# A decode step's backward pass: every engine's instruction order replaced, with four key/value gradient stores moved to GpSimd's queue

## Chip, core and metric

One core of one Trainium2 chip. The metric is the device time of one execution in microseconds (us); the kernel before has a median of 482.54 us in three runs (481.98 to 483.42).

## What is computed

The reference is the forward and backward pass of one decode step: an attention block with cached keys and values beside a gated bilinear block, both on the same normalised input of 2 rows (B = 2, D = 576).

```python
xn = _layernorm(x)
q = xn @ wq                                  # 32 query heads of 128, 16 key/value heads
p = softmax(q k^T * 128 ** -0.5)             # 4096 cached positions
out = x + (p v) @ wo + ((xn @ w_gate) * (xn @ w_up)) @ w_down
return out, *vjp(out)(grad_out)              # for x, k_cache, v_cache, wq, wo, w_gate, w_up, w_down
```

With one query per row there is little arithmetic. The caches are 32 heads of 1 MB each for keys and as many for values (bf16); they are read once, and their gradients, of the same size, are written once. The weights (576 x 4096, 4096 x 576, three of 576 x 4608) are read once, and their gradients written once.

## The kernel before

**Work.** A *step* `s` (16 of them) takes two key/value heads of one batch row: two K heads and two V heads are loaded, 1 MB each, into `big` tiles of 128 x 4096. A *group* is two steps (both batch rows of the same two heads); it needs a slice of `wq` and of `wo` and stores a slice of their gradients. Beside them run 9 *slices* of the bilinear block, 512 columns each, with loads of gate, up (tile `gu`, a single buffer) and down weights (tile `ww`).

In a step, by line: VectorE turns each head in blocks of 32 x 32 (`turn`, L421); TensorE forms the scores from K (`score`, L1105, t = 0), the softmax follows (L1171 to L1198), and V gives the gradient of the probabilities (L1105, t = 1) and from it the gradient of the scores (L1226 to L1237). GpSimd builds block-diagonal tiles `BD` from the query and from the gradient of the output (L1093, three buffers). `head_outer` multiplies them with the probabilities (dV, `out_3`) or with the score gradients (dK, `out_2`) on TensorE (L1127); each 128 x 1024 result is moved from PSUM by ScalarE (L425) or VectorE (L427), an *eviction*, and four of them fill a `big` tile, which one 1 MB DMA stores (`put`, L654). `contract` multiplies the probabilities with V and the score gradients with K (L1282). At a group's end `group_back` makes the gradients of `wq` and `wo` and adds to the sums `acc` and `accx` (L937, L962); after the last group `final_dx` turns `accx` into the input's gradient `out_1` (L1365 to L1389), and a DMA of 2 KB stores it (L1330).

**DMA.** Loads of K and V and of the down weights, and stores of dK and dV, are issued by SP (queue q1); the other weight loads and all stores of weight gradients by GpSimd, POOL in the profile (queue q0). The K and V loads of the last two steps are GpSimd's too. The two queues feed the same 16 DMA engines.

**Order.** The order of every engine's instructions is worked out by `Order` while the program is built. Each piece of work is a generator that asks for engines, buffers and DMAs, with a cost for each request; of the requests that can start within `SLACK` of the earliest on an engine, the one with the lowest priority number is taken. Priorities are `pr(name, s) = 28 s + PR[name]`, with offsets `HEAD` and `TAIL` for the first and last two steps. `EV` gives each eviction to ScalarE or VectorE, whichever would end first, with `BIAS` against VectorE. Class `Lines` models the two DMA queues as one server each, and `gate`s hold weight loads back until a given K or V load has been issued. The costs thus change nothing but the order: every wait on the chip is on a real semaphore, and an engine whose next instruction waits holds all that stand behind it. Each of the two kinds of queue has eight DMA semaphores, which its DMAs take in turn; an issue therefore also waits until the DMA eight before it has landed.

Of the kernel before, what the change touches and what calls it, by code (L numbers as in the profile page):

```python
# [52 lines left out]
class Lines:  # L53
# [5 lines left out]
    def run(self, until=None):  # L59
        line = self.line  # L60
        while (line[0] or line[1]) and (until is None or self.now < until):
            live, held = [], None
            for k in range(2):
                if line[k]:
                    x = line[k][0]
                    if not line[1 - k]:
                        x.hold = 0.0
                    if x.hold > 0:
                        held = x
                    else:  # L70
# [12 lines left out]
            for k in live:  # L83
                if line[k][0].work < 1e-9 or k == first:
                    line[k].pop(0).t = self.now + 1.4
# [19 lines left out]
class Order:  # L105
# [3 lines left out]
    def __init__(self):  # L109
        self.free = {e: 0.0 for e in ("PE", "ACT", "DVE", "POOL", "SP")}  # L110
        self.slots = {}
        self.home, self.cap, self.used = {}, {}, {}
        self.lines = Lines()
        self.quad, self.kind = (None, 0.0, 0.0), None
        self.streams = []
        self.count = 0
        self.log = []

# [44 lines left out]
    def start(self, s):  # L163
        r = s.req
# [19 lines left out]
        if r[0] == "dma":  # L184
            return max(s.ready, self.free[r[1]]), r[1]
# [7 lines left out]
    def run(self):  # L193
        while self.streams:
# [37 lines left out]
            elif r[0] == "dma":  # L232
                self.free[e] = t + r[2]
                s.land = self.lines.push(e == "POOL", t + r[2] + LATENCY[e], r[3], r[4])
                s.ready = t + r[2]
                self.log.append((t, r[2], e, s.gen.__name__))
# [43 lines left out]
def SPAWN(gen, prio):  # L280
    return ("spawn", gen, prio)
# [14 lines left out]
MLP0, MLPD = 0, 7.51  # L296
KVSTORE = "SP"
WQ0, WO0 = 0, 1
LATENCY, DRY = {"SP": 0.5, "ACT": 0.5, "POOL": 0.57}, 0.4
LM = 0.0  # L300
CLK = 2.0
BIAS = 0.52
SLACK = {"PE": 0.07, "ACT": 0.09, "DVE": 0.43, "POOL": 8.93, "SP": 17.19}
STEP = 28.0
HEAD = {"turn0": -27.5, "turn1": 17.9, "att": -70.5, "dsc": 20.0, "con": 10.4, "out1": 26.9, "out0": -42.2, "front": 26.2, "back": -304.6, "W0": 9.7, "W1": 90.3, "BD1": 30.3, "BD0": 91.5}
TAIL = {"turn0": 70.2, "turn1": -109.5, "att": -6.3, "dsc": -1.8, "con": -89.5, "conv": -4.6, "out1": -9.2, "out0": -5.8, "front": 37.9, "back": 9.6, "W1": -49.5, "BD1": 7.5, "BD0": -113.0, "load": -33.0}
PR = {"turn0": -74.6, "turn1": -110.6, "att": -719.4, "dsc": -725.3, "conv": 70.0, "con": -246.1, "out1": 1310.1, "out0": 250.5,
      "front": 190.0, "back": -43.0, "W0": 65.6, "W1": 62.0, "BD1": 442.2, "BD0": -91.5, "mlp": -115.0, "wout": -277.2,
      "store": 413.8, "load": -5.8, "wload": -723.6, "fin": 24.5, "const": 23.5, "mload": -44.2}
# [8 lines left out]
def kernel(  # L318
# [331 lines left out]
    def put(engine, parts, tag, slot, events=(), row=8192):  # L650
        def run():
            for j, (dst, src, nbytes) in enumerate(parts):
                yield DMA(engine, 0.78 if engine == "POOL" else 0.36, nbytes, row)
# [83 lines left out]
    def mlp(i, Lgu, Ld, gs_slot, wd_slot):  # L737
# [42 lines left out]
        po = pr("mlp", (MLP0 + i * MLPD) / 4) + PR["wout"]  # L780
# [204 lines left out]
    def load_kv():  # L985
        n = 0
        for s in range(NS):
            g, b = divmod(s, Bq)
            yield PRIO(pr("load", s))
            for t in range(2):  # L990
                for l in range(G):
                    i = yield ACQ("kv")
                    late = s > NS - 3
                    yield DMA("POOL" if late else "SP", 0.78 if late else 0.36, 1 << 20)
# [6 lines left out]
    def load_w(item):  # L1001
        kind, i = item
        if kind in ("wq", "wo"):
# [17 lines left out]
        else:  # L1021
# [4 lines left out]
            for w, Wsrc in enumerate((B_w_gate, B_w_up)):  # L1026
# [3 lines left out]
                yield DMA("POOL", 0.6, 64 * FS * 2, 4096)  # L1030
# [7 lines left out]
            yield SPAWN(mlp(i, Lgu, Ld, g, d), pr("mlp", (MLP0 + i * MLPD) / 4))  # L1038
# [76 lines left out]
    def head_outer(s, t, l, pr2, done):  # L1115
# [4 lines left out]
        store = Store(4, put(KVSTORE, [(oviews[t][b, G * g + l], st[:], 1 << 20)], "st", i, ()),  # L1120
# [235 lines left out]
    def final_dx():  # L1356
# [43 lines left out]
        (8 * g + WQ0, ("wq", g)), (8 * g + WO0 if g else 1, ("wo", g)))]), -50.0, 1.2)  # L1400
    od.spawn(load_ws([(MLP0 + i * MLPD, ("mlp", i)) for i in range(NFS)]), -50.0, 1.2)
# [36 lines left out]
```

## Time and profile before

| | |
|---|---|
| median of 3 runs | 482.54 us (481.98 to 483.42) |
| the profiled execution's own time, its span | 483.63 us, 481.8 us |
| granted TensorE clock, mean | 0.651 |
| busy share PE, DVE, ACT, POOL | 78%, 73%, 72%, 52% |
| bytes moved, of that from HBM and to HBM | 185.93 MB, 92.48 MB and 92.48 MB |
| eviction 128 x 1024 on ScalarE, on VectorE (busy time by count) | 254.8 us by 264, 53.4 us by 44 |
| turn of half a head, L421 | 1.22 us, 128 of them |
| building one BD tile on POOL, L1093 | 3.60 us, 32 of them |

The page gives the busy share of each engine, then the same in 40 slices; for the DMA engines it gives the mean busy share of the 16 and the bytes per second. A DMA share is the sum of the packets' own times; packets on one engine overlap a little, so the share of a full stretch is 1.02 and not 1. In the rows by group, "idle before" is the wait ahead of an instruction and what ended it; a wait on SP or POOL is charged to the queue's own sequencer.

### The profile page before, as it was taken

What the parts mean: (1) busy time and instruction counts of PE and PEld (TensorE: products, weight loads), DVE (VectorE), ACT (ScalarE), POOL (GpSimd) and SP (SyncE); (2) the same over time, 40 slices, a digit from 0 to 9 for tenths busy, and PEclk for the clock granted to TensorE, in tenths of its full rate; (3) what the DMA queues carried; (4) which work ended last, traced back from release to release, by engine and by line L of the source; (5) the groups of instructions that cost most, each with busy time, mean ns of one, the idle gap of its engine ahead of it and who ended that gap; (6) DMA issues with size and microseconds to landing.
All of it is one profiled execution on the core that took longest, in us unless ns stands there. A gap on an engine that the chain in (4) does not pass through costs nothing.

```text
span 481.8 us, 14584 instructions
## 1 busy us (share of the span) xinstructions
PE 377.4 (78%) x6122; PEld 213.5 (44%) x6122; DVE 350.0 (73%) x658; ACT 345.7 (72%) x529; POOL 248.6 (52%) x356
## 2 busy tenths in 40 slices
PE   0577977688852889879988997787797887599987
PEld 0444545443521554525553554444452545344544
DVE  6678856786747868677677878687686779398873
ACT  6059975598961688966758974799786973497993
POOL 6176803784146763451557624865715873265502
PEclk9999575666955666655555656667675665655695
DMA  8999999999999989999999999999999999999795
GB/s 298 387 402 327 414 396 422 384 379 388 423 414 373 389 335 333 400 419 398 415 399 409 366 394 422 397 413 421 411 392 421 420 416 395 402 403 375 280 407 198
DMA packets 33444, 185.93 MB, mean 386 GB/s; under 512 B 5034, under 2 KB 5170, under 8 KB 16994
## 3 DMA queue, kind: packets, MB, share of 16 engines
q1 hardware_dynamic: 18714, 131.22, 67.7%
q0 software_dynamic: 14656, 53.77, 29.7%
q8 instruction: 48, 0.79, 0.6%
q14 instruction: 18, 0.15, 0.1%
q10 hardware_dynamic: 8, 0.00, 0.0%
HBM read 92.48 MB, written 92.48 MB: 384 GB/s over the span
## 4 chain that ended last, share of the span: by engine, by line
DMA 37%; PE 29%; ACT 14%; DVE 10%; issue 5%; POOL 4%; SPq 0%; DVEq 0%; ACTq 0%; POOLq 0%
DMA out_dram<-big 23%; ACT big L425 11%; DMA gu<-in_B_w_up_dram 10%; PE ps_o L1127 6%; PE ps_m L1105 5%; PE ps_m L1282 5%; DVE big L421 4%; DMA gu<-in_B_w_gate_dram 3%; DMA big<-in_A_k_cache_dram 2%; POOL BD L1093 2%; DVE big L427 2%; PE ps_m L768 2%; PE ps_o L674 1%; PE ps_m L750 1%; PE ps_m L1193 1%
## 5 line engine op out<-in xcount | busy, mean ns | idle before, releaser
L425 ACT CAST big<-ps_o 128x1024 bf16<-128x1024 f32 (+1 forms) x324 | 288.2, 961 | 41.7 <-PE ps_o L1127 31.3
L421 DVE STREAM_TRANSPOSE big<-big 128x1024 f32<-128x1024 f32 x128 | 152.7, 1218 | 15.3 <-DMA out_dram<-big 10.8
L1093 POOL TENSOR_TENSOR BD<-vr,mask 128x2048 bf16<-128x2048 bf16 x32 | 115.3, 3602 | 31.2 <-ACT vr L425 16.6
L1105 PE MATMUL ps_m<-big,W 128*32 128x128 bf16 x2048 | 60.3, 285 | 9.6 <-POOL W L1070 4.8
L427 DVE CAST big<-ps_o 128x1024 bf16<-128x1024 f32 (+1 forms) x52 | 59.4, 1143 | 9.8 <-PE ps_o L1127 3.6
L1127 PE MATMUL ps_o<-BD,pp 32*128 32x512 bf16 x256 | 54.6, 544 | 14.1 <-ACT big L425 6.7
L1105 PEld LDWEIGHTS <-W 128*32 128x32 bf16 x2048 | 47.8, 127 | 28.4 <-issue 20.2
L654 POOL DMA_DIRECT2D out_dram<-big x43 | 33.4, 777 | 44.1 <-ACT big L425 26.5
L1070 POOL COPY W<-rep 32x16 bf16<-32x16 bf16 x128 | 24.5, 192 | 58.7 <-DVE rep L873 53.8
L1127 PE MATMUL ps_o<-BD,dd 32*128 32x512 bf16 x256 | 49.9, 530 | 6.0 <-ACT big L425 5.3
L421 DVE STREAM_TRANSPOSE big<-ww 128x1152 f32<-128x1152 f32 x25 | 34.0, 1359 | 7.6 <-DMA out_dram<-big 7.2
L1282 PE MATMUL ps_m<-big,pp 128*32 128x512 bf16 x256 | 32.1, 605 | 2.5 <-DVE accx L834 1.5
L1127 PEld LDWEIGHTS <-pp 32*128 32x128 bf16 x256 | 12.0, 99 | 37.3 <-issue 32.6
L625 POOL COPY wt<-wm 64x128 bf16<-64x128 bf16 (+1 forms) x34 | 8.9, 262 | 37.5 <-DVE wm L618 33.3
L1282 PE MATMUL ps_m<-big,dd 128*32 128x512 bf16 x256 | 26.7, 505 | 1.3 <-DVE hb L755 0.8
L421 DVE STREAM_TRANSPOSE big<-gu 128x1024 f32<-128x1024 f32 x18 | 21.8, 1223 | 3.0 <-DMA out_dram<-big 2.2
L1127 PEld LDWEIGHTS <-dd 32*128 32x128 bf16 x256 | 11.0, 99 | 26.6 <-issue 20.5
L654 POOL DMA_DIRECT2D out_dram<-tl x26 | 14.4, 557 | 15.9 <-ACT tl L425 6.6
L632 PE MATMUL ps_m<-big,wm 128*32 128x128 bf16 x416 | 13.8, 293 | 9.1 <-DVE big L421 7.9
L1292 ACT ACTIVATE osb<-ps_m 128x512 bf16<-128x512 f32 x15 | 9.1, 606 | 15.7 <-PE ps_m L1282 15.7
L674 PEld LDWEIGHTS <-xnr 32*128 32x128 bf16 x416 | 15.2, 117 | 8.3 <-issue 6.9
L674 PE MATMUL ps_o<-hb,xnr 32*128 32x128 bf16 x288 | 17.0, 271 | 2.3 <-ACT big L425 0.7
(210 smaller groups left out, 561.4 us busy)
## 6 DMA issues: line engine op xcount, KB each, us to landing
out_dram<-big SPq DMA_DIRECT2D x64, 1024.0 KB, 11.3
big<-in_A_k_cache_dram SPq DMA_DIRECT2D x28, 1024.0 KB, 12.7
big<-in_A_v_cache_dram SPq DMA_DIRECT2D x28, 1024.0 KB, 17.2
out_dram<-big POOLq DMA_DIRECT2D x26, 512.0 KB, 11.7
out_dram<-big POOLq DMA_DIRECT2D x17, 576.0 KB, 9.5
ww<-in_B_w_down_dram SPq DMA_DIRECT2D x9, 576.0 KB, 15.0
ww<-in_A_wo_dram POOLq DMA_DIRECT2D x8, 576.0 KB, 14.3
gu<-in_B_w_gate_dram POOLq DMA_DIRECT2D x9, 512.0 KB, 13.0
```

Of the source, the lines that this page charges most:

```text
L421: nc.vector.transpose(out, in_)
L425: nc.scalar.copy(out, in_)
L427: nc.vector.tensor_copy(out=out, in_=in_)
L632: nc.tensor.matmul(dp[32 * q:32 * q + 32, 0:P], lhsT=view(Wm[:], 0, P, 8 * pos(q, s), [[1, 32]]), rhs=view(X, 0, P, xoff(q, s), [[xstep, 4 ...
L654: (nc.gpsimd if engine == "POOL" else nc.sync).dma_start(dst, src)
L674: nc.tensor.matmul(o[:, aa, dc * P:(dc + 1) * P], lhsT=xnr[32 * a:32 * a + 32, dc * P:(dc + 1) * P], rhs=rhs(a), start=True, stop=True)
L768: nc.tensor.matmul(dh, lhsT=Wdy[:, e, 2 * k:2 * k + P], rhs=view(X[:], 0, P, 64 * k + e, [[D, FC], [2, 32]]), start=(k == 0 and e == 0), s ...
L1070: nc.gpsimd.tensor_copy(view(W_t[t][w][:], 32 * a, 32, 6 + 8 * a, [[G * WW, 4], [WW, G], [1, 2]]), view(rep_t[grp[g]["qs"]][:], 32 * a, 32 ...
L1093: nc.gpsimd.tensor_tensor(BD_t[i][:], view(vr_t[v][:], 0, P, 0, [[0, 16], [1, Dh]]), view(mask16[:], 0, P, 0, [[1, 16], [0, Dh]]), ALU.mult)
L1105: nc.tensor.matmul(sc[32 * cq:32 * cq + 32, :], lhsT=view(W[:], 0, P, (be * G + l) * WW + 6 - 4 * c2 - 2 * l, [[1, 32]]), rhs=view(X[:], 0 ...
L1127: nc.tensor.matmul(o[:, k, :], lhsT=pr2[32 * c4:32 * c4 + 32, :], rhs=BD[32 * c4:32 * c4 + 32, 8 * l + 4 * h2:8 * l + 4 * h2 + 4, :], star ...
L1282: nc.tensor.matmul(ct[32 * j:32 * j + 32, :], lhsT=view(rT, 0, P, 4 * c + 2 * l, [[1, 32]]), rhs=kv_t[kvS[s][t][l]][:, Dh * c:Dh * (c + 4) ...
```

## The change

No computation, buffer or transfer size is changed, save that each 64 KB rest of `wq` is loaded by two DMAs of 64 rows in place of one of 128. What changes is: the planner's DMA costs, a lane rule (a DMA may not be planned before the eighth DMA ahead of it has landed), all priorities, a table `OFF` that shifts single steps, the places at which the weight loads are let go (`MLP_AT`, `WQ_AT`, `WO_AT`), `BIAS` and `SLACK`, and the engine that issues the four dK and dV stores of step 14 (`POOL_STORES`), which is now GpSimd.

```diff
-            return max(s.ready, self.free[r[1]]), r[1]
+            lanes = self.lanes["SW" if r[1] == "POOL" else "HW"]
+            return max([s.ready, self.free[r[1]]] + [when(x) for x in lanes[-8:-7]]), r[1]
...
 def DMA(engine, cost, nbytes, row=8192):
-    packet = 0.0375 * row + 9.0
-    return ("dma", engine, cost, 0.08 + nbytes / 16e3 * packet / row, packet)
+    packet = 0.0364 * row + 8.0
+    return ("dma", engine, cost, 0.02 + nbytes / 16e3 * packet / row, packet)
...
-MLP0, MLPD = 0, 7.51
-KVSTORE = "SP"
-WQ0, WO0 = 0, 1
+OFF = {"mload": {2: 138.2}, "wload": {13: 2.1}, "BD1": {1: -144.5}, "out1": {6: -20.1}, "turn1": {8: -38.6},
+       "conv": {13: -250.2}, "front": {11: -29.3}}
+POOL_LOADS, POOL_STORES = [28, 29, 30, 31], [28, 29]
+MLP_AT = [0.93, 10.84, 15.91, 23.4, 30.89, 38.38, 45.87, 53.36, 60.85]
+WQ_AT = [-1, 8, 16, 24, 32, 40, 48, 56]
+WO_AT = [3, 9, 18, 26, 34, 40, 50, 58]
...
-BIAS = 0.52
-SLACK = {"PE": 0.07, "ACT": 0.09, "DVE": 0.43, "POOL": 8.93, "SP": 17.19}
+BIAS = 0.407
+SLACK = {"PE": 0.1, "ACT": 0.11, "DVE": 0.44, "POOL": 1.03, "SP": 17.19}
...
-    return STEP * s + PR[name] + edge.get(name, 0)
+    return STEP * s + PR[name] + edge.get(name, 0) + OFF.get(name, {}).get(int(s), 0)
...
             if kind == "wq":
-                yield DMA("POOL" if i else "SP", 0.6, 128 * 256 * 2, 4096 if i else 512)
-                (nc.gpsimd if i else nc.sync).dma_start(ww_t[w][:, 4 * FS:WB],
-                                                        A_wq[512:576, n0:n0 + FS].rearrange("p (h n) -> h p n", h=2))
+                for h in range(2):
+                    yield DMA("POOL" if i else "SP", 0.55 if i else 0.36, 64 * 256 * 2, 2048 if i else 512)
+                    (nc.gpsimd if i else nc.sync).dma_start(ww_t[w][64 * h:64 * h + 64, 4 * FS:WB],
+                                                            A_wq[512:576, n0 + 256 * h:n0 + 256 * h + 256])
...
-        store = Store(4, put(KVSTORE, [(oviews[t][b, G * g + l], st[:], 1 << 20)], "st", i, ()),
+        store = Store(4, put("POOL" if 2 * s + t in POOL_STORES else "SP", [(oviews[t][b, G * g + l], st[:], 1 << 20)], "st", i, ()),
                       pr(f"out{t}", s))
```

`HEAD`, `TAIL` and `PR` get new numbers throughout. The loads that GpSimd issues are the same as before (`POOL_LOADS` names the last two steps).

More of the change, by code (lines that the diff above doesn't have):

```diff
@@ L84, in run @@
                 if line[k][0].work < 1e-9 or k == first:
-                    line[k].pop(0).t = self.now + 1.4
+                    line[k].pop(0).t = self.now + LAG
     def push(self, k, at, work, packet):
@@ L117, in __init__ @@
         self.log = []
+        self.lanes = {"HW": [], "SW": []}
     def ring(self, tag, n):
@@ L234, in run @@
                 s.land = self.lines.push(e == "POOL", t + r[2] + LATENCY[e], r[3], r[4])
+                self.lanes["SW" if e == "POOL" else "HW"].append(s.land)
                 s.ready = t + r[2]
@@ L299 @@
+POOL_LOADS, POOL_STORES = [28, 29, 30, 31], [28, 29]
+MLP_AT = [0.93, 10.84, 15.91, 23.4, 30.89, 38.38, 45.87, 53.36, 60.85]
+WQ_AT = [-1, 8, 16, 24, 32, 40, 48, 56]
+WO_AT = [3, 9, 18, 26, 34, 40, 50, 58]
 LATENCY, DRY = {"SP": 0.5, "ACT": 0.5, "POOL": 0.57}, 0.4
-LM = 0.0
+LM, LAG = 0.0, 1.4
 CLK = 2.0
-BIAS = 0.52
-SLACK = {"PE": 0.07, "ACT": 0.09, "DVE": 0.43, "POOL": 8.93, "SP": 17.19}
+BIAS = 0.407
+SLACK = {"PE": 0.1, "ACT": 0.11, "DVE": 0.44, "POOL": 1.03, "SP": 17.19}
 STEP = 28.0
-HEAD = {"turn0": -27.5, "turn1": 17.9, "att": -70.5, "dsc": 20.0, "con": 10.4, "out1": 26.9, "out0": -42.2, "front": 26.2, "back": -304.6, "W0": 9.7, "W1": 90.3, "BD1": 30.3, "BD0": 91.5}
@@ L306 @@
[L306 to L309, printed above, removed]
+HEAD = {"turn0": -25.2, "turn1": -31.7, "att": -70.5, "dsc": 195.5, "con": 9.5, "out1": 26.9, "out0": 94.5,
+        "front": 26.2, "back": -376.6, "W0": -16.3, "W1": 64.8, "BD1": 30.3, "BD0": 91.5, "conv": -75.9,
+        "load": -114.3}
@@ new lines @@
+TAIL = {"turn0": 43.7, "turn1": 86.0, "att": 110.3, "dsc": 0.2, "con": -89.5, "conv": 36.8, "out1": -9.2,
+        "out0": 33.2, "front": -529.0, "back": -358.1, "W1": 39.2, "BD1": -22.9, "BD0": -120.6, "load": 281.8}
+PR = {"turn0": -84.8, "turn1": -110.6, "att": -681.0, "dsc": -724.2, "conv": 70.0, "con": -230.8, "out1": 1310.1,
+      "out0": 250.5, "front": 164.9, "back": -70.9, "W0": -353.3, "W1": 70.5, "BD1": 442.2, "BD0": -91.5,
+      "mlp": -130.5, "wout": -278.8, "store": 413.2, "load": -6.5, "wload": -718.4, "fin": -57.5, "const": 5.5,
+      "mload": -58.3}
@@ L652, in run @@
             for j, (dst, src, nbytes) in enumerate(parts):
-                yield DMA(engine, 0.78 if engine == "POOL" else 0.36, nbytes, row)
+                yield DMA(engine, 0.36 if engine != "POOL" else 0.55 if nbytes < 1 << 17 else 0.78, nbytes, row)
                 (nc.gpsimd if engine == "POOL" else nc.sync).dma_start(dst, src)
@@ L779, in mlp @@
         E = [Event() for _ in range(4)]
-        po = pr("mlp", (MLP0 + i * MLPD) / 4) + PR["wout"]
+        po = pr("mlp", MLP_AT[i] / 4) + PR["wout"]
         yield SPAWN(rows_outer(lambda a: hb[32 * a:32 * a + 32, 0, :],
@@ L992, in load_kv @@
                     i = yield ACQ("kv")
-                    late = s > NS - 3
-                    yield DMA("POOL" if late else "SP", 0.78 if late else 0.36, 1 << 20)
+                    late = 2 * s + t in POOL_LOADS
+                    yield DMA("POOL" if late else "SP", 0.55 if late else 0.36, 1 << 20)
                     (nc.gpsimd if late else nc.sync).dma_start(kv_t[i][:], views[t][b, G * g + l])
@@ L1029, in load_w @@
                                   Wsrc[0:512, f0:f0 + FS].rearrange("(c p) n -> p c n", p=P))
-                yield DMA("POOL", 0.6, 64 * FS * 2, 4096)
+                yield DMA("POOL", 0.55, 64 * FS * 2, 4096)
                 nc.gpsimd.dma_start(gu[64 * w:64 * w + 64, 8 * FS:9 * FS], Wsrc[512:576, f0:f0 + FS])
@@ L1037, in load_w @@
             yield ("lset", Ld)
-            yield SPAWN(mlp(i, Lgu, Ld, g, d), pr("mlp", (MLP0 + i * MLPD) / 4))
+            yield SPAWN(mlp(i, Lgu, Ld, g, d), pr("mlp", MLP_AT[i] / 4))
     def load_ws(items):
@@ L1399 @@
     od.spawn(load_ws([it for g in range(NG) for it in (
-        (8 * g + WQ0, ("wq", g)), (8 * g + WO0 if g else 1, ("wo", g)))]), -50.0, 1.2)
-    od.spawn(load_ws([(MLP0 + i * MLPD, ("mlp", i)) for i in range(NFS)]), -50.0, 1.2)
+        (WQ_AT[g], ("wq", g)), (WO_AT[g], ("wo", g)))]), -50.0, 1.2)
+    od.spawn(load_ws([(MLP_AT[i], ("mlp", i)) for i in range(NFS)]), -50.0, 1.2)
     od.spawn(load_kv(), 0.0, 1.2)
```

## The prediction

> **What bounds the kernel now.** First the page's DMA part: what the 16 engines did in 40 slices of 12 us, and by queue.
>
> ```profile
> DMA  8999999999999989999999999999999999999795
> GB/s 298 387 402 327 414 396 422 384 379 388 423 414 373 389 335 333 400 419 398 415 399 409 366 394 422 397 413 421 411 392 421 420 416 395 402 403 375 280 407 198
> q1 hardware_dynamic: 18714, 131.22, 67.7%
> q0 software_dynamic: 14656, 53.77, 29.7%
> ```
>
> The transfers fill nearly the whole span, and the bytes don't change. So the question is only where the DMA engines stand idle. The windows view answers it (us; PE, PEld, DVE, ACT, POOL busy; granted clock, DMA share, GB/s):
>
> ```profile
> 0.00:12.00 12.00, 1.02 (x8) 0.46 (x8) 7.50 (x36) 7.64 (x12) 8.18 (x24) 1.00 0.83 297
> 36.00:46.00 10.00, 7.15 (x138) 4.29 (x139) 9.29 (x17) 9.71 (x16) 6.04 (x5) 1.00 0.88 308
> 140.00:182.00 42.00, 25.14 (x433) 15.01 (x436) 28.54 (x46) 22.71 (x36) 25.13 (x27) 0.58 0.96 371
> 182.00:432.00 250.00, 208.47 (x3300) 115.28 (x3292) 183.27 (x323) 186.73 (x288) 133.10 (x195) 0.60 1.02 402
> 432.00:458.00 26.00, 23.76 (x354) 12.46 (x353) 22.19 (x40) 23.11 (x34) 14.80 (x11) 0.63 0.84 334
> 458.00:470.00 12.00, 10.40 (x178) 5.14 (x177) 8.65 (x18) 12.00 (x16) 0.89 (x3) 0.93 1.00 410
> 470.00:481.80 11.80, 8.30 (x86) 5.48 (x84) 3.69 (x13) 3.96 (x7) 2.29 (x4) 0.50 0.50 191
> ```
>
> From 182 to 432 us the DMA share is 1.02 at 402 GB/s: full, and nothing on another engine matters there. At that rate the 185.93 MB take 462.5 us of the 481.8. The lost 19.3 lie in the other windows; (1.02 - share) / 1.02 x length gives 2.2 (start), 1.4 (36 to 46), 2.5 (140 to 182), 4.6 (432 to 458) and 6.0 us (the end), 16.7 in all. These five places are what an order can win or lose.
>
> Why 140 to 182? POOL's and SP's timelines (start, us, engine, line, in brackets the idle time and what ended it):
>
> ```profile
> 141.34 0.55 POOL L654 DMA_DIRECT2D out_dram<-tl  x1 [2.21 <-DMA out_dram<-big]
> 144.86 0.53 POOL L654 DMA_DIRECT2D out_dram<-tl  x1 [2.97 <-DMA out_dram<-big]
> 147.33 0.82 SPq L654 DMA_DIRECT2D out_dram<-big  x2
> ```
>
> Two 64 KB stores on POOL wait 5.2 us for earlier DMAs to land, the eight-semaphore turn that the old planner didn't know; SP, whose last issue was at 127.68, stands until 147.33 before a store, with two loads behind it. The old order ran into waits that it had not planned.
>
> Why 432 to 470? The chain of waits is DMA for 37% of the span, but in its last 50 us it is made of TensorE, ScalarE and VectorE pieces. The last V load was issued at 422.06 (by the row of DMA issues) and landed 19.0 us later, at 441; VectorE turned it only at 453:
>
> ```profile
> big<-in_A_v_cache_dram POOLq DMA_DIRECT2D x1, 1024.0 KB, 19.0
> 453.14 2.33 DVE L421 STREAM_TRANSPOSE big<-big 128x1024 f32<-128x1024 f32 x2
> 473.26 0.32 DVE L962 TENSOR_TENSOR accx<-accx,ps_m 128x160 f32<-128x160 f32 x1 [0.99 <-PE ps_m L637]
> ```
>
> So the load was 12 us early, and the tail waits for compute. From the turn to the last addition to `accx` it is 20.1 us, from there to the end 8.5.
>
> **The change, part by part.** The sum is made against the profiled execution (483.63 us, span 481.8) and carried as a difference to the median, 482.54.
>
> *Start.* In SP's program the two halves of the first `wq` rest now stand ahead of the first K load; before, the load was issued at 0.74 us and the rest behind it took 0.69. The K load comes one to two such issues later, 0.7 to 1.4 us; some of it is covered, since the same 64 KB then no longer stand between the first two K heads. If covered wholly it costs nothing. I take +0.8, near the single issue that the trace shows.
>
> *36 to 46 us.* GpSimd's three loads for group 1 were issued from 36.05, behind two BD builds; now they stand ahead of the second, 3.6 us (one build) earlier, and so 1.15 MB comes when the engines ran dry. Against it, the loads behind SP's first two stores still wait for those stores' evictions, as before. Between all of the 1.4 us won and 1 lost to the later start, I take -0.5.
>
> *140 to 182 us.* The new planner counts the turn of eight, but 7 more small loads and 4 stores enter POOL's turn. Between all of the 2.5 us won and as much lost to new waits, nearer to the first, as the waits seen are of the kind now counted: -1.5.
>
> *182 to 432 us.* Full before; 0 as long as it stays full. POOL gets 7 issues of 0.55 us, at 52% busy. ScalarE hands VectorE six 128 x 1024 and four 128 x 576 evictions (counted in the two programs): ScalarE -6 x 0.965 - 4 x 0.59 = -8.2 us, VectorE +6 x 1.214 + 4 x 0.75 = +10.3, to 75% of the span. Hidden by the transfers here; it helps from 458 to 470, where ScalarE is busy 12.00 of 12 us and VectorE 8.65.
>
> *The stores moved to POOL.* 4.19 MB go from q1 to q0. By share per MB q0 costs 0.552% against q1's 0.516; if all of that were the queue and not its smaller packets, 4.19 x 0.036% x 481.8 = 0.7 us; 0 taken, as for packets of one size the difference should vanish. Behind the first two stores stands the last BD build (before: 455.01 to 458.6, first used at about 462.3, so 3.7 us of cover); the second of them was issued at 456.42 from SP, and a build behind it would end at 460.8, still covered by 1.5 us.
>
> *Tail.* The two programs list all engines' instructions in one sequence; I compare them where 170.46 MB of DMAs have been issued (the last V load after). Before: 321 large evictions, 218 turns, 5381 matmuls. After: 321, 223 and 5465. So the new order is five turns (5 x 1.22 = 6.1 us of VectorE) and 84 matmuls further, at equal bytes. From 422 on TensorE did 757 matmuls in 59.8 us, so 84 are 6.6 us of it; on VectorE and ScalarE, busy together 92.3 us of these 59.8, 6.1 us are 3.0 of the pair. I take the smaller, -3.0: evictions bind the tail, TensorE waits for them. Three of the evictions (one dV store of step 15) now stand behind the addition to `accx`, beside `final_dx`: about two on ScalarE, 1.9 us, off the path. But the 1 MB store they fill leaves some 3 us after that addition, and the tail's SP stores land 6.5 us after issue in the median; 3 and 6.5 are 9.5, one more than the 8.5 that `final_dx` needs, so of the 1.9 won 0.9 remain, taken as -0.8. Tail: -3.8, between -8 (most of the 10.6 us lost there) and +5 (the rival below).
>
> Sum: +0.8 - 0.5 - 1.5 - 3.8 = **-5.0 us**, so 478.6 for a profiled execution and **477.5 us** for the median.
>
> A rule that speaks of the room for this: the Trainium skill, DMA: Bandwidth & Descriptors, section Bandwidth, puts the ceiling of the DMA path at 435 GB/s and says that for HBM transfers the memory side, about 358 GB/s, binds. By 435 the bytes would need 427 us and an order could win up to 54; by 358 they would need 519, more than the kernel takes. The trace agrees with neither: 402 GB/s in the full stretch.
>
> **Rivals.**
>
> *Nothing to win:* the holes move, and what one place gains another gives back, because the engines are full for 250 us and a shifted load only shifts its hole. For it: 97.4% of the span is already packets. Against: the tail's holes are compute's, and the tail has less compute left. 481.1 to 484.0 us.
>
> *The last V load comes too late (slower).* Before it stood on POOL directly behind two other loads, at 422.06. Now it stands behind a BD build and three stores of weight gradients, whose evictions are number 318 to 321; before, number 321 was stored at 427.2, so the load goes out at about 428. With 19.0 us it lands at 447; the tail, 5 us shorter, wants to turn it at 448. One microsecond of cover is left of 12. From there each microsecond is the end's: turn, scores, dK, `group_back` and `final_dx` follow in one chain of 28.7 us. GpSimd's DMAs of that stretch landed up to 23.2 us after issue (a gate or up load); a POOL that stalls 6 us more on an eviction or a semaphore turn puts the landing at 457 and the end at 457 + 28.7 = 485.7, about 486.5 as a median. For it: POOL waited 26.8 us in all ahead of such stores. Against: fewer bytes are queued ahead of the load now, so that it should land sooner than 19 us.
>
> *All holes close:* start kept, 36 to 46 and 140 to 182 filled, the tail as the TensorE count has it (-6.6): -0.3 - 1.4 - 2.5 - 6.6 = about -10, so 472.
>
> *The change does nothing:* can't be; the programs differ on every engine.
>
> **How the numbers follow.** Chances: forecast (474 to 481) 0.54, all holes close (below 474) 0.13, nothing to win (481.1 to 484) 0.11, late load or another new wait (above 484) 0.22. About 0.3%, 1.4 us, is what a measurement of this kernel can tell from no change: faster 0.67, same 0.11, slower 0.22. The range from 470.5 to 486.5 holds the late load's price and all but the deepest gain. The forecast's own range is 474 to 481.
>
> **What would show it.** In the after profile: DMA share above 0.84 from 432 us to 12 us before the end; the first K load issued at 1.4 to 2.1 us; no POOL wait of over 2 us on a DMA's landing between 140 and 182; the full stretch still at about 402 GB/s; the chain's last part without a DMA wait for the last V load; `accx` finished some 4 us earlier than 473.3. It would be wrong if a full stretch lost rate (below 395 GB/s is 4 us), or if the chain names the last V load or POOL's queue in its last 40 us.

## The result, and the profile after

| | before | after |
|---|---|---|
| median us (executions, lowest to highest) | 482.03 (20, 479.70 to 486.41) | 485.39 (20, 482.84 to 486.86) |
| the profiled execution, its span | 483.63, 481.8 | 484.26, 482.5 |
| granted clock, mean | 0.651 | 0.667 |

The ratio is 1.0059 (95% interval 1.0039 to 1.0078): **slower by 0.6%**, 3.4 us, where 477.5 and a gain were predicted. One caution for all that follows: single executions of one kernel lie 4 to 7 us apart, and the two profiled ones, 483.63 and 484.26, differ by 0.6 us in time and 0.7 in span. The trace of before comes from an execution that is slow for its kernel, that of after from one that is fast for its own. So the two traces explain where 0.7 us went and where the predicted gain went; the other 2.7 us of the medians' difference are in neither.

The page of after, DMA part (40 slices of 12 us, then queues with packets, MB and share):

```profile
DMA  7999799999999999999999999999999979996896
GB/s 281 383 410 409 233 409 415 407 368 417 417 415 403 411 419 393 405 421 418 420 395 420 423 420 420 405 414 410 404 403 419 383 238 404 388 407 256 313 375 261
q1 hardware_dynamic: 18168, 127.02, 64.6%
q0 software_dynamic: 14672, 57.94, 31.5%
```

Five slices are below 300 GB/s: the first, the fifth (48 to 60 us), the 33rd (386 to 398), the 37th (434 to 446) and the last. The fifth and the 33rd were full before. The windows of after (columns as in the prediction):

```profile
0.00:12.00 12.00, 1.02 (x8) 0.56 (x9) 7.88 (x37) 7.64 (x12) 8.18 (x24) 1.00 0.76 280
36.00:46.00 10.00, 7.58 (x114) 5.33 (x115) 9.45 (x17) 3.77 (x7) 0.00 (x0) 0.66 1.02 405
46.00:60.00 14.00, 12.90 (x237) 7.68 (x236) 10.76 (x24) 11.13 (x20) 11.70 (x13) 0.58 0.78 264
140.00:182.00 42.00, 33.96 (x622) 18.34 (x621) 36.28 (x62) 31.91 (x46) 30.38 (x42) 0.67 1.02 410
182.00:384.00 202.00, 157.54 (x2629) 88.45 (x2630) 151.66 (x267) 139.81 (x214) 99.53 (x143) 0.63 1.01 412
384.00:408.00 24.00, 20.50 (x394) 12.16 (x382) 18.45 (x36) 20.47 (x31) 17.65 (x25) 0.76 0.83 305
432.00:458.00 26.00, 21.40 (x348) 12.26 (x341) 20.75 (x38) 20.08 (x28) 17.63 (x13) 0.63 0.76 295
458.00:470.00 12.00, 11.07 (x104) 3.73 (x101) 8.32 (x14) 11.31 (x15) 2.72 (x6) 0.50 0.91 371
470.00:482.50 12.50, 8.75 (x74) 4.99 (x73) 4.84 (x14) 3.92 (x6) 1.78 (x3) 0.50 0.71 268
```

By the prediction's formula, (1.02 - share) / 1.02 x length, after loses 3.1 us at the start, 3.3 at 46 to 60, 4.5 at 384 to 408, 6.6 at 432 to 458, 1.3 to 470 and 3.8 at the end: 22.6 in all, where before lost 16.9 in its own places. Two of the old holes (36 to 46, 140 to 182) are gone, two new ones are there. The 5.7 us more are nearly paid for by the rate of the full stretch: 412 GB/s where before had 402 in the same 202 us, and 202 x 10 / 402 is 5.0 us. The rest, 0.7, is the difference of the spans.

Where do the new holes come from? At 46 to 60, POOL's timeline shows it:

```profile
33.11 0.76 POOL L1029 DMA_DIRECT2D ww<-in_A_wo_dram  x1
48.14 0.63 POOL L635 COPY wt<-wm 64x128 bf16<-64x128 bf16 x2 [14.27 <-DVE wm L628]
48.86 3.60 POOL L1104 TENSOR_TENSOR BD<-vr,mask 128x2048 bf16<-128x2048 bf16 x1
```

The weight loads were put ahead of the second BD build, and behind them a copy of `wt` for which POOL stands 14.27 us. So the build that was at 32.50 before is now at 48.86, and the first dK matmuls, which read it, start at 53.24 and not 39.59, with their evictions behind them; ScalarE is busy 3.77 of the 10 us to 46. Between 39 and 52.4 us no store is issued, and at 50 the loads run out.

At 384 to 408, VectorE's waits and timeline (us in total, times, longest; then one instruction):

```profile
DVE big L431 <- DMA out_dram<-big: 29.3, 16, 5.3
DVE big L431 <- DMA ww<-in_B_w_down_dram: 8.5, 3, 5.9
...
DVE big L431 <- DMA big<-in_A_k_cache_dram: 4.5, 4, 2.0
```

```profile
376.23 1.38 DVE L431 STREAM_TRANSPOSE big<-ww 128x1152 f32<-128x1152 f32 x1 [5.90 <-DMA ww<-in_B_w_down_dram]
```

Turns wait for landings: of stores (their tile is to be written again) and of loads. Before, the first row was 20.2 us by 10. The rows of DMA issues between 182 and 345 us say why landings are late; the last number is the median from issue to landing, first before, then after:

```profile
out_dram<-big SPq DMA_DIRECT2D x23, 1024.0 KB, 14.6
big<-in_A_k_cache_dram SPq DMA_DIRECT2D x12, 1024.0 KB, 12.3
...
out_dram<-big POOLq DMA_DIRECT2D x9, 512.0 KB, 12.2
```

```profile
out_dram<-big SPq DMA_DIRECT2D x24, 1024.0 KB, 21.6
...
big<-in_A_k_cache_dram SPq DMA_DIRECT2D x10, 1024.0 KB, 20.7
out_dram<-big POOLq DMA_DIRECT2D x9, 512.0 KB, 12.7
```

SP issues its loads earlier than before, with the engines already full: by 0 to 20 us, 7 in the median of the 31 K and V loads that SP issued between 150 and 380 us. They wait in SP's queue, and so does everything issued behind them: from issue to landing it takes 6 to 8 us more (V loads 22.8 and not 17.2). POOL's 512 KB stores are as fast as they were; of its loads, those of `wq` and `wo` land 2 us sooner and the two or three of gate and up 4 to 5 us later. The Trainium skill, DMA: Bandwidth & Descriptors, section Queues, rings and completion order, has each DMA engine change between the queue rows packet by packet; a row served by turns and a backlog in the other agrees with 21.6 beside 12.7 us.

The lead that the early loads make is real and worth nothing. Counted in the traces: at 384 us after has moved 153.6 MB, before 150.7; but after has done 311 evictions and issued 101 stores, before 317 and 102. So the 3 MB are loads. From 384 to 396 after moves 2.5 MB, before 5.0, and at 396 the two stand at 156.1 and 155.7.

The end (chain of waits of after: start, us, what):

```profile
412.41 20.14 DMA big<-in_A_k_cache_dram
...
432.57 2.52 DVE big L431 x2
```

This is the last K head, issued by POOL. It lands at 432.55 and is turned at once. Before, it landed at 432.5 too, but VectorE turned it only at 441.7: 9 us of cover, now none. What stands behind that turn has become longer: 49.9 us to the end, before 40.1, and 39.0 to 41.1 in every kernel here with before's last part, where the head lies 9 to 13 us before it is turned. Counted in the traces, 50 evictions and 514 matmuls start behind the turn, before 43 and 489. So the new order spends before's cover on a longer end, and with the head landing at the same time it gains nothing.

The last V head is turned 3.5 us sooner than before (449.65 for 453.14), but `accx` is finished at the same time (before at 473.26):

```profile
449.65 1.20 DVE L431 STREAM_TRANSPOSE big<-big 128x1024 f32<-128x1024 f32 x1
473.59 0.32 DVE L972 TENSOR_TENSOR accx<-accx,ps_m 128x160 f32<-128x160 f32 x1 [0.52 <-PE ps_m L647]
```

Between these two 31 evictions start, before 25, and they take 23.9 us and not 20.1. The turns were put forward, and evictions were left behind them.

### The profile page after: what moved, and what is told of

Same layout as the page of the kernel before. It is cut to its first block, busy times and chain, and to the rows that moved or that the text cites. A ratio compares the mean times of both kernels' runs of the same rounds, so it can differ in the third digit from the quotient of the medians.

```text
span 482.5 us, 14613 instructions
## 1 busy us (share of the span) xinstructions
PE 373.1 (77%) x6122; PEld 210.6 (44%) x6122; DVE 362.0 (75%) x679; ACT 335.5 (70%) x508; POOL 252.3 (52%) x367
## 5 line engine op out<-in xcount | busy, mean ns | idle before, releaser
L435 ACT CAST big<-ps_o 128x1024 bf16<-128x1024 f32 (+1 forms) x314 | 279.9, 956 | 50.7 <-PE ps_o L1138 33.9
L437 DVE CAST big<-ps_o 128x1024 bf16<-128x1024 f32 (+1 forms) x62 | 69.6, 1123 | 10.6 <-PE ps_o L1138 5.7
L1138 PE MATMUL ps_o<-BD,pp 32*128 32x512 bf16 x256 | 47.6, 536 | 9.5 <-ACT big L435 5.5
L664 POOL DMA_DIRECT2D out_dram<-big x47 | 35.7, 760 | 36.8 <-ACT big L435 25.3
L1293 PE MATMUL ps_m<-big,dd 128*32 128x512 bf16 x256 | 30.6, 581 | 12.0 <-DVE accx L972 6.4
L1081 POOL COPY W<-rep 32x16 bf16<-32x16 bf16 x128 | 24.7, 193 | 20.2 <-DVE rep L883 15.1
L1138 PEld LDWEIGHTS <-dd 32*128 32x128 bf16 x256 | 11.4, 99 | 25.8 <-issue 20.4
L1138 PEld LDWEIGHTS <-pp 32*128 32x128 bf16 x256 | 9.8, 99 | 25.3 <-issue 22.0
L1303 ACT ACTIVATE osb<-ps_m 128x512 bf16<-128x512 f32 x12 | 7.3, 610 | 18.4 <-PE ps_m L1293 15.6
L778 PE MATMUL ps_m<-big,Wdy 128*128 128x128 bf16 x162 | 15.8, 274 | 3.3 <-DVE big L431 2.6
L684 PE MATMUL ps_o<-hb,xnr 32*128 32x128 bf16 x288 | 14.1, 248 | 5.2 <-ACT big L435 4.6
## 6 DMA issues: line engine op xcount, KB each, us to landing
big<-in_A_v_cache_dram SPq DMA_DIRECT2D x28, 1024.0 KB, 20.2
ww<-in_B_w_down_dram SPq DMA_DIRECT2D x9, 576.0 KB, 24.6
ww<-in_A_wo_dram POOLq DMA_DIRECT2D x8, 576.0 KB, 12.7
```

Source lines behind the costliest of these rows:

```text
L435: nc.scalar.copy(out, in_)
L437: nc.vector.tensor_copy(out=out, in_=in_)
L664: (nc.gpsimd if engine == "POOL" else nc.sync).dma_start(dst, src)
L684: nc.tensor.matmul(o[:, aa, dc * P:(dc + 1) * P], lhsT=xnr[32 * a:32 * a + 32, dc * P:(dc + 1) * P], rhs=rhs(a), start=True, stop=True)
L778: nc.tensor.matmul(dh, lhsT=Wdy[:, e, 2 * k:2 * k + P], rhs=view(X[:], 0, P, 64 * k + e, [[D, FC], [2, 32]]), start=(k == 0 and e == 0), s ...
L1081: nc.gpsimd.tensor_copy(view(W_t[t][w][:], 32 * a, 32, 6 + 8 * a, [[G * WW, 4], [WW, G], [1, 2]]), view(rep_t[grp[g]["qs"]][:], 32 * a, 32 ...
```

## Experiments

Every kernel was timed in five rounds; "before" in their ratios is the kernel before on the same chip at the same time. In all but one the planner's picks (4152 in the changed kernel) were recorded and played back, so that each has the order of after on every engine, or that of before where it is said, except for the edit shown; a_oldrate plans anew. The line numbers are those of after. The *theories* at the start were: the holes at 0, 46 and 384 us, each with one local cause, cost the end what they last (so mending one shows at the end); or the engines are full on both sides of a hole and mending it only shifts it.

**The three holes, one by one and together.** The start: the first K load again ahead of the two halves. 46 to 60: the second BD build ahead of POOL's loads, its evictions and stores ahead of the first weight gradients'. 384: VectorE doesn't wait for the late down weights (and TensorE's 18 matmuls with them come behind one contraction).

```diff
 SP (a_fixA)
+L1005 DMACopy big_61<-in_A_k_cache_dram 128x4096
 L1020 DMACopy ww_79<-in_A_wq_dram 64x256 x2
-L1005 DMACopy big_61<-in_A_k_cache_dram 128x4096
...
 POOL (a_fixB)
+L1104 TensorTensor BD_87<-vr_90,mask_205 128x2048
 L1020 DMACopy ww_82<-in_A_wq_dram 64x256 x2
 L1024 DMACopy ww_82<-in_A_wq_dram 128x4x512
 L1029 DMACopy ww_83<-in_A_wo_dram 128x4x576
 L635 TensorCopy wt_105<-wm_103 64x128 x2
-L1104 TensorTensor BD_87<-vr_90,mask_205 128x2048
...
 DVE (a_fixC)
-L431 StreamTranspose big_69<-ww_79 128x1152
 L431 StreamTranspose dd_120<-sp_134 128x256
 L972 TensorTensor accx<-accx,ps_m_150 128x160
 L431 StreamTranspose big_74<-big_71 128x1024 x2
 L431 StreamTranspose big_63<-big_64 128x1024
+L431 StreamTranspose big_69<-ww_79 128x1152
```

> The changed kernel's order, instruction for instruction, with one edit: on SP the first K load is issued ahead of the two wq halves, as in the kernel before. Local theory (each hole of the changed kernel is one misplaced instruction, and filling it brings its length): the DMA engines start 1.2 us sooner and the end comes 1 us sooner, 484.4 us against 485.4. Drift theory (the order was planned for transfers of 441 us, where they need 462, so transfers land up to 24 us later than planned, and what is gained at one place is lost at the next late landing): under 0.5 us, 485 us.

> The changed kernel's order with one block moved: the second BD build of the first step and the evictions and stores of its dK stand where the kernel before has them, ahead of the first weight-gradient evictions, so that the hole of 3.2 us at 50 to 54 us should close. Local theory: 3 us less than the changed kernel, 482.4 us. Drift theory: the loads behind are late in any case, the time stays within 1 us of the changed kernel's 485.4.

> The changed kernel's order with one step moved: the transposes of the eighth slice's w_down, for which VectorE stood 5.9 us at 370.3, come behind the dd transposes, the accx sum and three K transposes that waited behind them, and the eight matmuls that read those transposes come behind one more contraction. Local theory: VectorE's 5.9 us shrink below 1.5, the hole of 4.4 us at 382 to 392 closes, and the end comes 3 to 4 us sooner, 481.5 to 482.5 us. Drift theory: that wait goes, but the next transfer lands as late as before, and less than 1.5 us of it reach the end, 484 us or more.

> The three moves of the runs beside it together. Local theory: the sum, 7 to 8 us less than the changed kernel, 477.5 to 478.5 us, faster than both kernels. Drift theory: 2 us at most, 483.5 us or more.

| | median us | ratio to before |
|---|---|---|
| a_fixA | 485.39 | 1.0058 (1.0028 to 1.0088) |
| a_fixB | 489.56 | 1.0159 (1.0119 to 1.0200) |
| a_fixC | 485.36 | 1.0047 (1.0010 to 1.0084) |
| all three | 489.40 | 1.0156 (1.0115 to 1.0197) |

None gains anything that can be told from noise; the intervals are 1.5 to 2 us to either side. A gain of 0.7 us from the start alone could hide in them; the 3 to 8 us that the local theory asked of the others could not. The windows of a_fixA (start mended, 384 not; its trace is of the slowest of its executions):

```profile
0.00:12.00 12.00, 1.02 (x8) 0.56 (x9) 7.95 (x37) 7.64 (x12) 8.17 (x24) 1.00 0.82 307
...
384.00:408.00 24.00, 22.07 (x406) 11.79 (x402) 18.98 (x37) 21.48 (x33) 16.70 (x24) 0.66 0.79 285
```

In this trace the 0.7 us won at the start, 0.06 x 12 / 1.02, stand beside a hole at 384 that is deeper by 0.04 x 24 / 1.02 = 0.9; a single execution doesn't show that the one caused the other. a_fixB fills 46 to 60 from 0.78 to 0.90 (1.6 us), but from 60 to 140 its share is 0.97 with 369 GB/s, where after has 1.01 with 406: 3 us lost by share, more by rate. (Behind the edit some uses in a_fixB take other tiles, and ScalarE has three evictions more; by what the tiles are worth, further down, that may be part of its loss.) In a_fixC the wait of 5.90 us went, and the next turn waits for a V load, issued at 353.93 and landed 27.2 us later:

```profile
381.13 1.25 DVE L431 STREAM_TRANSPOSE big<-big 128x1024 f32<-128x1024 f32 x1 [5.53 <-DMA big<-in_A_v_cache_dram]
```

So the hole at 384 isn't that one load's: the transfer that stands next is late as well.

**Fewer bytes to store.** If the order's own dependences bind, a lighter DMA load leaves after's losses in place; if the queue's backlog does, they shrink. The 64 stores of dK and dV leave out the last 512 of 4096 columns (8.4 MB of 185.9 less), in the order of after and in that of before:

```diff
-[(oviews[t][b, G * g + l], st[:], 1 << 20)]
+[(oviews[t][b, G * g + l][:, 0:3584], st[:, 0:3584], 7 << 17)]
```

> The changed kernel's order, with less to move: each of the 64 stores of a dK or dV tile leaves out the last 512 of its 4096 columns, 8.4 MB of 186, worth 21 us at the 402 GB/s of the full stretches; all computation stays. Drift theory (the order is good for transfers as quick as its planner takes them, 441 us of work in all, and loses on the chip because they take 462): now transfers take what the plan has for them, landings come on time, and this order is faster than the order of before with the same bytes left out, by 4 us or more: 464 us against 468. Order theory (the order itself starves the engines, whatever the transfers take): it stays the slower of the two, by 3 us or more, 471 us against 467.

> The order of the kernel before, with the same 8.4 MB of dK and dV left out of the stores as in the run beside it; all computation stays. Drift theory: this order has transfers of 471 us planned into it and gains less from lighter ones, 468 us. Order theory: it gains more than the changed order does, 467 us or less against 471.

a_light: 469.72 us, ratio 0.9745 (0.9715 to 0.9775). b_light: 470.34, 0.9756 (0.9731 to 0.9780). With less to move the two orders are within 0.1% of each other. At 402 GB/s the bytes left out are 20.9 us; after won 15.7 of them, before 11.7. So after's order gains 3 to 4 us more from the lighter load than before's (3.4 by the ratios, 4 by the medians). That fits a loss by backlog, but neither theory had the result: the drift theory wanted a lead of 4 us for after, the order theory one of 3 us for before, and they come out level. A limit outside the DMA that both meet would level them too; no run tells the two apart. The hole at 384 is gone in a_light (the share is 0.99 from 372 to 396 us too, where the shorter kernel would have it):

```profile
384.00:408.00 24.00, 15.82 (x268) 8.66 (x269) 16.39 (x28) 15.02 (x26) 13.20 (x24) 0.71 1.02 398
```

The turns' waits for stores fall from 29.3 to 18.7 us, with before's order from 20.2 to 11.4. The hole behind 432 is still there and comes earlier with the shorter kernel: at 420 to 432 us the share is 0.62, in after 0.68 at 444 to 456.

**The four stores back on SP.**

```diff
-POOL_LOADS, POOL_STORES = [28, 29, 30, 31], [28, 29]
+POOL_LOADS, POOL_STORES = [28, 29, 30, 31], []
```

> The changed kernel's order with the four dK and dV stores that the change moved to GpSimd's queue back on SP's, at their places in the order; nothing else differs. If that move costs (POOL issues them behind two BD builds and a copy), the end comes 1 us or more sooner than the changed kernel's, 484 us or less; if it helps, 486.5 or more (SP's stores stand behind one that waits 27 us); drift and order theories both say no difference, 485 to 486 us.

485.16 us, 1.0063 (1.0040 to 1.0085): the same as after. What the move to GpSimd's queue costs or brings is less than the 1.5 us that these runs can tell.

**The planner's old DMA constants under the new priorities.**

```diff
-    packet = 0.0364 * row + 8.0
-    return ("dma", engine, cost, 0.02 + nbytes / 16e3 * packet / row, packet)
+    packet = 0.0375 * row + 9.0
+    return ("dma", engine, cost, 0.08 + nbytes / 16e3 * packet / row, packet)
```

> The changed kernel with the transfer times of the planner as they were before (0.0375 a byte and 9.0 a packet, 0.08 us a transfer in place of 0.0364, 8.0 and 0.02); priorities, shifts and the rest stay as changed, and the order is planned anew. If the quick transfer times by themselves make the order bad, this is faster than the changed kernel, 480 to 483 us. If the priorities and shifts fit only the transfer times that they were searched with, so that any other planning scrambles the order, it is slower than both, 490 us or more.

497.59 us, 1.0331 (1.0306 to 1.0355). So the old constants don't mend the order: under them the new priorities and shifts make one that is 12 us slower still. The two belong together, and what the constants alone do can't be read from this run.

**Which half?** after's order for the first 3168, 2756 or 1632 steps of its plan (some 360, 315 and 185 us of its trace) and before's behind it, and the reverse. The tiles behind the seam have to be chosen anew.

> The first 3168 of the changed planner's 4152 steps in the changed order (to about 360 us of its trace), all that is left in the order of the kernel before, with its engines and queues. At 360 us the changed kernel's DMA engines have moved 143.5 MB, the other's 140.5, 7 us at 402 GB/s. Late-part theory (the change gains in its first three quarters and loses it all in its own last 120 us): the gain is kept, 475 to 477 us, faster than both kernels. Borrowed-lead theory (the lead is transfers taken early, which is paid back in any order behind it): 481 to 484 us.

> The same with the seam at 2756 steps, some 315 us of the changed kernel's trace; there its lead is 3.0 MB as well (127.3 MB against 124.3 at 320 us). Late-part theory: 475 to 477 us again. Borrowed-lead theory: 481 to 484 us.

> The same with the seam at 1632 steps, some 185 us of the changed kernel's trace, where its lead is 0.8 MB, 2 us (70.3 MB against 69.5 at 182 us): the holes at 36 to 46 and 140 to 182 us are closed in this part, and the one at 50 is opened. Late-part theory: 479.5 to 480.5 us. Borrowed-lead theory: 482 us.

> The reverse: the first 3047 steps in the order of the kernel before (to some 351 us of its trace), the rest in the changed order, with its stores on POOL. Late-part theory: no lead is won and the changed end is kept, which loses 5 us or more against the end of before: 487 to 490 us, slower than both kernels. Borrowed-lead theory: with no early loads to pay back the changed end is as good as the other, 480 to 483 us.

483.95 (1.0013, 0.9982 to 1.0044), 487.52 (1.0101, 1.0070 to 1.0132), 490.97 (1.0165, 1.0100 to 1.0231); reverse, 489.04 (1.0123, 1.0068 to 1.0179). Read plainly: after's first three quarters with before's end are as good as before, with no lead kept, as the borrowed-lead theory had it; after's end behind before's start is bad, as the late-part theory had it. But the seam disturbs. In ab180 VectorE stands 13.65 us for a tile whose store hasn't landed; the longest such wait in after is 5.3 us, in before 6.3:

```profile
391.33 1.38 DVE L431 STREAM_TRANSPOSE big<-ww 128x1152 f32<-128x1152 f32 x1 [13.65 <-DMA out_dram<-big]
```

In ab300 the longest is 10.8 us. In ab345 there is one of 6.24 us at 383, just behind the seam, which neither kernel has at that place. ab300 and ab180 therefore settle nothing, and the two others were run once more with other tiles.

**The tiles alone.** Each engine's order stays after's; only which of the 16 `big` tiles a use gets is chosen anew, by the landing times in the trace of after (222 of 269 uses change). Then the two seams in the same way.

> The changed kernel's order, every engine's instructions as they are; only which of the 16 tiles each load, transposes and store uses is chosen anew, as the one that comes free first by the landing times of the changed kernel's trace, where the planner chose by its own, too early ones (222 of 269 uses change). By these times the waits for tiles sum up to 137 us with the planner's choice and to 93 with the new one. If wrongly chosen tiles are what the quick transfer times cost, 2 us or more are won, 483.4 or less; if it is the order, no change, 484.5 to 486.

> The changed order up to 3168 steps and the order of before behind it once more, with tiles behind the seam chosen by the traces' landing times (in the run before, VectorE stood 6.2 us at 385 for a tile whose store had not landed, a wait that neither kernel has). Late-part theory: the lead of 7 us at 360 us is kept, 475 to 478 us. Borrowed-lead theory: 481 us or more.

> The order of before up to 3047 steps and the changed order behind it, tiles behind the seam chosen by the traces' landing times. Late-part theory: the changed end costs 5 us or more, 487 us or more. Borrowed-lead theory: 480 to 484 us.

a_slots: 482.59 us, 0.9989 (0.9959 to 1.0020). Against after that is 0.9930, about 0.0036 to either side: a gain of 0.7%, with the same instructions in the same order. The hole at 384 is nearly gone, that behind 432 isn't:

```profile
384.00:408.00 24.00, 19.99 (x380) 11.37 (x374) 17.71 (x35) 19.52 (x31) 16.43 (x22) 0.72 0.98 367
432.00:458.00 26.00, 21.26 (x344) 12.26 (x341) 20.93 (x38) 20.12 (x28) 17.70 (x13) 0.63 0.73 285
```

Its profiled execution, 484.18 us, is the slowest of its twelve, so the trace doesn't show where the gain lies; VectorE's waits for stores are even longer in it than in after's, 36.2 us for 29.3. ab345s gives 486.87 (1.0098, 1.0065 to 1.0130) and ba345s 486.19 (1.0084, 1.0058 to 1.0110): with other tiles the first becomes worse and the second better than its twin, by 0.9 and 0.4%. The new choice didn't take the tiles out of the question: in ab345s the same wait behind the seam is 12.04 us, twice that of ab345. After's end behind before's start is slower than before with either choice; beyond that, what a half is worth is no larger than what its tiles are worth, and the question "which half" has no clear answer here.

**Is that a rule?** The same choice made for before's order, by the trace of before (219 of 269 uses; the `wq` rests as two DMAs as in after).

> The control to the run with newly chosen tiles: the order of the kernel before, with its tiles chosen anew in the same way from its own trace's landing times (219 of 269 uses change; the small wq loads go in two halves, as in the changed kernel). By these times its waits for tiles sum up to 57 us with the planner's choice, to 36 with the new one. Tile theory (the changed kernel loses 3.4 us because its planner took landings for too early and chose tiles that come free late): the order of before was planned with slower transfers and has little to win, within 1.5 us of before, 480.5 to 483.5 us. If choosing by the trace helps any order alike: 3 us or more, 479 us or less.

484.88 us, 1.0054 (1.0032 to 1.0076): worse, which neither theory had. VectorE's longest wait for a store is 8.9 us, before 6.3. So the choice by one trace's landings is no rule; it moves the time by about half a per cent, to either side.

**Shorter queue on SP.** If SP's backlog delays the down weights, POOL's queue brings them sooner:

```diff
-            yield DMA("SP", 0.36, 128 * FC * D * 2, 4608)
-            nc.sync.dma_start(ww_t[d][:, 0:FC * D].rearrange("p (c n) -> p c n", c=FC),
+            yield DMA("POOL", 0.78, 128 * FC * D * 2, 4608)
+            nc.gpsimd.dma_start(ww_t[d][:, 0:FC * D].rearrange("p (c n) -> p c n", c=FC),
```

> The changed kernel's order with one queue changed: the nine loads of w_down slices are issued by POOL, right behind the gate and up loads of their slice, and no longer by SP. From 182 to 345 us SP's transfers of the changed kernel land 21 to 23 us after their issue (14.6 to 17.2 for before), POOL's 10 to 13 in both. Queue theory (the order issues K and V earlier into SP's queue, which serves in order, so all that is behind them on SP lands late and VectorE, in order, stands for it): w_down lands within 15 us, VectorE's wait of 8.5 us for it goes, and the time falls by 2 us or more, to 483.4 or less. If any engine's next late landing just takes its place, as where the one transposes were moved: no change, 485 us.

They land 17.3 us after issue in the median, not 24.6, and VectorE's wait for them falls from 8.5 to 2.9 us. The kernel takes 486.23 us (1.0085, 1.0054 to 1.0116), no faster, and within noise of after. Waits of a_wdpool:

```profile
POOL ww L1046 <- DMA out_dram<-big: 9.7, 2, 5.2
...
PE ps_m L1293 <- DMA big<-in_A_v_cache_dram: 6.1, 1, 6.1
...
DVE big L431 <- DMA big<-in_A_v_cache_dram: 5.2, 1, 5.2
```

POOL now stands 9.7 us for the landing of stores ahead of two of these loads (the turn of eight semaphores), and a V head is late where the down weights were.

**The end.** a_slots with the last slice's work (transposes, matmuls, its stores on SP) put behind evictions and a K turn that the end needs:

```diff
 PE
-L778 Matmult ps_m_150<-big_62,Wdy 128x128 x18
 L1310 Matmult ps_m_151<-fold,osb_122 128x4 x4
 L1138 Matmult ps_o<-BD_87,pp_118 128x512 x6
+L778 Matmult ps_m_150<-big_62,Wdy 128x128 x18
```

> The changed order with newly chosen tiles, and two edits in its last 50 us: the matmuls of the last MLP slice (they read w_down's transposes of 433.5 us) come behind three dV evictions that stood behind them ready, with one K transposes ahead of the product on VectorE; and that slice's stores of gradients are issued by SP, which stands idle there, and not by POOL behind a BD build and a copy. ACT stood idle for 4.5 us at 433.2 and the DMA engines for 5.5 us at 440 to 447. If the end is set by the evictions of the last 45 us (ACT is busy for 11.3 of 12 us at 458 to 470), they start 2 to 3 us sooner: 479.5 to 480.5 us, faster than both kernels. If the next late piece takes the place of this wait, as before: 482 to 483 us.

484.20 us, 1.0030 (1.0005 to 1.0054): no gain over a_slots. ScalarE's gap of 4.5 us at that place becomes two of 2.04 and 2.73 us, and the end comes 51.7 us after the last K turn and not 50.0.

No version that stores everything beats both kernels; a_slots ties with before.

**Across the runs: the last K head.** In the profiled executions of all kernels that have after's last part:

| | last K head landed | span | from there |
|---|---|---|---|
| after | 432.5 | 482.5 | 50.0 |
| a_fixA, a_fixB | 434.5, 438.0 | 484.5, 488.0 | 50.0, 50.0 |
| a_fixC, all three | 433.8, 436.7 | 483.7, 486.7 | 49.9, 50.1 |
| a_spstores | 434.9 | 484.1 | 49.2 |
| a_slots, ba345, ba345s | 432.3, 437.8, 437.8 | 482.3, 486.9, 488.0 | 50.0, 49.1, 50.2 |
| a_light | 418.6 | 467.6 | 49.0 |
| a_wdpool, a_slots_end | 434.5, 430.4 | 486.7, 482.6 | 52.2, 52.2 |

The landing varies by 19 us (by 8 without a_light) and the rest by 3. With this end the time moves with the landing of one load, and some 50 us follow. (In a_wdpool the head lies 2.4 us before its turn, and 49.8 us follow that turn.) Before, it is 49.3 us from landing to end too, but 9 of them are cover. And issuing it earlier doesn't land it earlier: before issued it at 414.19 and it took 18.3 us, after at 412.41 and 20.1, a_slots at 408.69 and 23.6 us, and all three land within 0.3 us of each other. The others with after's last part and all bytes issue it between 410 and 419 us and land it between 430 and 438 in no order; a_wdpool, the last to issue it, lands it at 434.5.

## Why the prediction was wrong

The measured 485.39 lies inside the range; the sign is wrong. By its steps:

- **Start, +0.8.** Right as a size: the share went from 0.83 to 0.76, 0.8 us. Whether it reaches the end can't be seen: a_fixA took it back, and the kernel stayed at 485.39, to within 1.5 us.
- **36 to 46 us, -0.5.** The hole closed as said and another of 3.3 us opened at 46 to 60. The step priced three loads and left out what they were moved ahead of: a BD build, and behind it dK's matmuls, its evictions and the first stores, 13.7 us later. Giving the old order back in this one place didn't help either (a_fixB, 489.56).
- **140 to 182 us, -1.5.** Right: full, 2.5 us won, POOL's wait for a landing 0.3 us.
- **182 to 432 us, "0 as long as it stays full".** Failed: it didn't stay full (0.83 at 384 to 408, 4.5 us). The step took the share for a property of that stretch. It lasts only while loads and stores are ready, and the new order had its loads done early and its evictions 6 behind (311 for 317 at 384 us). Its mean of 400 GB/s, above the 395 that was named as the sign of trouble, hides this: 412 for 202 us and then 305 for 24. The sign should have been asked of slices.
- **Stores on POOL, 0.** Right (a_spstores).
- **Tail, -3.8, the largest term.** Failed. That the new order is "five turns and 84 matmuls further, at equal bytes" was counted in the programs at an equal count of bytes issued, and the same count had the large evictions level, 321 and 321. The step says that evictions bind the tail and yet takes its lead from the turns. The last V turn did come 3.5 us sooner, but with 31 evictions between it and `accx` and not 25, and the 20.1 us that were carried over from before became 23.9. Nor was the lead in bytes landed: the new order issues earlier and lands at the same time. At 432 us after has moved 170.4 MB and done 359 evictions, before 170.0 and 356. The three evictions' lead is gone by 452 (378 against 379). `accx` came at 473.59 and not 4 us before 473.26, and the share from 432 to 470.5 was near 0.81 where "above 0.84" was predicted. (Two slips in this step's working: 6.1 us of work on a pair that is busy 92.3 us in 59.8 are 4.0 us, not 3.0; and the trace has 737 matmuls from 422 us on, not 757. The first would have made the forecast lower still.)
- **The rival on the other side** had the right kind and the wrong load. The last V load was issued at 426.57 (428 said), landed at 448.3 (447 said), and was turned 1.3 us later (1 said). But cover had run out 16 us before it on the same queue, at the last K head, which the prediction never looked at. With 50 us from its landing to the end, it is what the time moves with, as the table shows. The chain of waits names that DMA at 412 to 432 us, 10 us ahead of the "last 40 us" that the prediction set as its sign. The measured time falls in the class that it shared with "another new wait", above 484, which had 0.22.
- "What one place gains another gives back" had 0.11 and a range that ended at 484.0. The experiments on single holes go with it: two moved the time by less than their intervals, and a_fixB gave back more than it won.
- **What the sum left out.** It compares orders and has no term for which `big` tile a use gets. The same order with other tiles (a_slots) gains 0.7%, about all that after lost. (The working of "all holes close" adds up to -10.8, not -10; the 472 given there is right.)

The prediction weighed a rule on rates: the Trainium skill, DMA: Bandwidth & Descriptors, section Bandwidth, lets about 358 GB/s bind for transfers between HBM and SBUF, and its table of single-core numbers has 425 for 16 MB. After's full stretch ran at 412 on one core, near the second figure and above the first.

**What stays open.** Which part of the medians' 3.4 us the traces don't show (2.7 us of it): it would need the traces of typical executions of both. (The profiled executions of a_fixA, a_fixC and a_spstores, kernels close to after, took 485.6 to 486.3 us, and in them the last K head lands 1.3 to 2.4 us later than in after's trace; that is a hint and no more.) Why a_slots's tiles win 0.7% and b_slots's lose 0.5%. Whether either half of the new order is good by itself: the seams cost as much as the halves differ. That the last K head's landing sets the end is shown by twelve kernels in which the two move together, not by a run that moved that load alone: whatever delays all transfers would move both.

## What to carry to other kernels

Where the DMA engines were full, as here, a load issued earlier was a loan: it waited longer in its queue, what stood behind it in that queue landed later too, and the hole came back when there was nothing left to load; so count what has *landed* and what was *stored*, not what was issued. In the last 50 us ask of each late load, on each queue, how long its data lie there before they are used, and how much work stands behind that use: the first one without cover is where the end begins to move with the transfers. And where buffers wait for their stores, which buffer a use gets is a part of the order, worth here (0.7%) as much as a whole new order of every engine (0.6%).

## What was not expected of the hardware

- At one DMA share (1.01 to 1.02) the two kernels' full stretches moved 412 and 402 GB/s. The 8 KB packets on q1 took 318 ns each in the mean, not 325. What makes them shorter is open.
- With both queues busy, 1 MB on SP's queue took 12 to 17 us before and 21 to 23 in after (182 to 345 us), stores of 512 KB on GpSimd's 12.2 and 12.7: these stores hardly felt the other queue's backlog. (GpSimd's gate and up loads took 10.4 and 14.4 us before, 15.3 and 18.6 in after, but these are medians of three and of two.) The first K head, on empty engines, took 5.7 us.
- The 20 executions of after, at a granted clock of 0.65 to 0.70, lie 4.0 us (0.8%) apart, those of before 6.7 us; a trace is one of them, and a difference of 0.7% can't be read from two.
